# Last ten MLP blocks: layer one in 49 products for 1280 tokens at a time, layer two summed in four steps

## The chip, the cores and the metric

The kernel runs on one NeuronCore of one Trainium2 chip. The metric is the device time of the core in microseconds (us). The kernel before took 1379.85 us, the median of three runs (1377.99 to 1382.92). Engine names in the profile: PE is TensorE (PEld its weight loads), DVE VectorE, ACT ScalarE, POOL GpSimd, SP SyncE, which here issues DMAs.

## The reference

Two blocks follow each other, all in float32. The first is attention over 8 batches, 8 heads, 576 positions and 64 dimensions per head, in which scores below the row's maximum less tau are dropped:

```python
scores = scale * np.matmul(q, k.transpose(0, 1, 3, 2))
thresh = np.max(scores, axis=-1, keepdims=True) - tau
scores = np.where(scores >= thresh, scores, -1000000000.0)
...
attn = attn / (np.sum(attn, axis=-1, keepdims=True) + 1e-09)
return np.matmul(attn, v).astype(np.float32)
```

Its output, as 4608 tokens by 512, goes through a two-layer MLP with an exact gelu:

```python
h = x @ w_in                                   # 512 -> 2048
g = 0.5 * h * (1.0 + erf(h * inv_sqrt2))
return (g @ w_out).astype(np.float32)          # 2048 -> 512
```

## The kernel before

The tokens are cut into 18 blocks of 256 (TOK). Attention runs by pairs of heads, 32 pairs in all. Beside it, between the pieces of attention, the first eight blocks (PLAIN) go through the MLP with ordinary products: `block_steps` multiplies w_in by the block's x (L559), takes a gelu on ScalarE and multiplies by w_out (L573). x is held with the 512 model channels on the partitions, as four chunks c of 128; chunk c comes from the c-th pair of heads of a batch. `weigh_v` (L469) makes x from the attention weights and v, and `divide` (L502), on GpSimd, divides it by the softmax sums, whose reciprocals (inv) come back by DMAs that SP issues. Order is written out by hand (`manual_schedule`): each engine runs its instructions in the order in which the Python program issues them.

The last ten blocks run after attention, in `strassen` (L664). Five of them (AWAY, blocks 8 to 12) are finished early and are parked in DRAM by `put_away`, others stay in SBUF; `bring` loads a parked block back. Two blocks at a time (DUOS) go through both layers with seven products in place of eight (the scheme of Strassen in Winograd's form): each matrix is cut into 2 x 2 quarters, sums of quarters are multiplied, and the products are added up.

- Sums of w_in quarters (s1, s2, s4) are made once, on VectorE, before the stage (`weights_in`, L622, L633 to L635 and L641). Sums of x quarters (t1, t2, t4) are made for each pair on VectorE (`x_sums`, L659 to L662), those of w_out while the first pair runs (`w_out_sums`, L704 to L707).
- Layer one: for each of eight chunks j of 128 of the 1024 columns in a half of d_ff, seven products of two matmuls, 256 tokens wide. All matmuls of the stage are recorded at L693, in `product`. Products that belong together are added in one PSUM bank: the bank x takes m1, then m6, m5 and m3 on top, and after each of them ScalarE or VectorE copies the bank's state out before the next is added. The bank y takes m7 and then m4, the bank v_ takes m2.
- Gelu on ScalarE, then the sums gs1, gs2 and g11 - g21 on VectorE (`finish_chunk`).
- Layer two: the same seven products, each over all eight j, for two chunks m of 128 tokens, then DMAs of 128 x 256 to the output.

Both layers are float32; each matmul shows in the trace as two passes, a weight load and a matmul each. The x, w_in and w_out tiles are many tiles in pools before, and one tensor each after.

## Time and profile before

| what | value |
|---|---|
| median of three runs | 1379.85 us (1377.99 to 1382.92) |
| profiled execution: its own time, which is its span | 1380.0 us, 20235 instructions |
| mean granted TensorE clock | 0.995 |
| TensorE busy | 99% of the span |
| last ten blocks | 889.35 us to the end, 490.65 us |
| in these: TensorE, VectorE, ScalarE, GpSimd busy | 484.96, 149.36, 126.64, 1.69 us |
| one pair of blocks between two stalls | 96.97 us, 448 passes |

The page gives one profiled execution, on the one core. The span is all that the page shows of its time; it stands 0.15 us from the median of the runs. A duration of an operation is its busy time; engines other than TensorE start the next operation somewhat before the last one's end, so the pitch of two starts is shorter than the duration. The granted clock in the last ten blocks is 1.00.

### The profile page before, as it was taken

The page shows a single profiled execution, that of the slowest core. Times are in us where ns is not written, and L with a number is a line of the kernel's source. Part 1 is how long each engine was busy: PE and PEld are TensorE (multiplying, and loading weights), DVE is VectorE, ACT ScalarE, POOL GpSimd, SP SyncE. Part 2 cuts the span into 40 slices and gives each one's busy share as a digit, 9 for nine tenths or more (in the row PEclk, how much of TensorE's full clock was granted, in tenths as well). Part 3 has the DMA queues.
Part 4 walks back from the last instruction along what each step waited for, and adds up shares of the span by engine and source line. Part 5 has one row for each costly group of instructions (what it writes and reads, how often), then busy time and mean ns, then how long its engine had stood idle before and what let it go on. Part 6 is the DMA issues. An engine that isn't in the chain of part 4 may idle for free.

```text
span 1380.0 us, 20235 instructions
## 1 busy us (share of the span) xinstructions
PE 1361.4 (99%) x6734; PEld 971.0 (70%) x6734; DVE 892.6 (65%) x1740; ACT 638.0 (46%) x1160; POOL 435.6 (32%) x896
## 2 busy tenths in 40 slices
PE   9899999999999999999999999999999999999999
PEld 7677557466466566576475475588888888888887
DVE  7998777788888888888888888763142242241330
ACT  7766537448348358357367366241240230330420
POOL 5553344454554554554555551100000000000000
PEclk9999999999999999999999999999999999999999
DMA  9987366577677687787787775500000001001000
GB/s 295 313 301 222 80 162 140 139 167 175 157 176 171 157 198 163 161 213 158 167 219 156 169 180 116 111 0 8 23 1 27 19 1 47 15 0 54 9 8 23
DMA packets 215094, 169.19 MB, mean 123 GB/s; under 512 B 114176, under 2 KB 199488, under 8 KB 214992
## 3 DMA queue, kind: packets, MB, share of 16 engines
q1 hardware_dynamic: 191040, 112.84, 36.1%
q0 software_dynamic: 23520, 54.77, 13.1%
q8 instruction: 55, 0.90, 0.3%
q14 instruction: 47, 0.39, 0.1%
q10 hardware_dynamic: 432, 0.30, 0.1%
HBM read 72.73 MB, written 12.52 MB: 62 GB/s over the span
## 4 chain that ended last, share of the span: by engine, by line
PE 95%; DVE 2%; ACT 1%; DMA 1%; issue 0%; POOL 0%; ACTq 0%; DVEq 0%
PE bank L693 35%; PE hT L559 17%; PE o_ps L573 17%; PE sc L367 13%; PE xT L484 11%; PE tr L309 2%; DMA raw<-in_moe_w_in_dram 1%; DVE p L398 1%; ACT p L382 0%; DVE nmx L379 0%; DVE power L187 0%; DVE w_in L189 0%; PE tr L280 0%; ACT diag L412 0%; PE idle L125 0%
## 5 line engine op out<-in xcount | busy, mean ns | idle before, releaser
L382 ACT ACTIVATE p<-sc,nmx 128x576 f32<-128x576 f32 x288 | 201.8, 737 | 268.8 <-DVE nmx L379 268.7
L398 DVE SCALAR_TENSOR_TENSOR p<-sc,thr,p 128x576 f32<-128x576 f32 x288 | 225.4, 816 | 60.0 <-ACT p L382 58.8
L379 DVE TENSOR_REDUCE nmx<-sc 128x1 f32<-128x576 f32 x288 | 205.6, 751 | 66.2 <-PE sc L367 65.6
L559 PE MATMUL hT<-x,w_in 128*128 128x256 f32 x1024 | 241.1, 385 | 0.0
L573 PE MATMUL o_ps<-w_out,g 128*128 128x512 f32 x512 | 237.7, 605 | 0.0
L559 PEld LDWEIGHTS hT<-x,w_in 128*128 128x128 f32 x1024 | 189.8, 190 | 48.9 <-issue 23.5
L380 POOL TENSOR_SCALAR thr<-nmx,tau_eff 128x1 f32<-128x1 f32 x288 | 89.0, 309 | 390.4 <-DVE nmx L379 390.0
L573 PEld LDWEIGHTS o_ps<-w_out,g 128*128 128x128 f32 x512 | 93.5, 191 | 111.0 <-issue 109.4
L484 PE MATMUL xT<-pT,v 128*64 128x256 f32 (+1 forms) x1280 | 164.0, 409 | 0.2 <-issue 0.2
L367 PE MATMUL sc<-kT,qT 64*128 64x288 f32 x960 | 157.2, 431 | 2.4 <-DVE p L398 1.9
L445 DVE STREAM_TRANSPOSE turned_p<-p 128x1152 f32<-128x1152 f32 x112 | 154.4, 1378 | 3.9
L367 PEld LDWEIGHTS sc<-kT,qT 64*128 64x128 f32 x960 | 89.5, 187 | 75.7 <-issue 64.3
L484 PEld LDWEIGHTS xT<-pT,v 128*64 128x64 f32 x1280 | 89.1, 137 | 72.7 <-issue 13.3
L693 PE MATMUL bank<-x,w_in 128*128 128x256 f32 x480 | 116.7, 379 | 0.0
L693 PE MATMUL bank<-w_out,unit 128*128 128x256 f32 x520 | 115.5, 379 | 0.0
L234 POOL DMA_DIRECT2D v<-in_v_dram x208 | 110.9, 536 | 4.5 <-issue 2.5
L693 PEld LDWEIGHTS bank<-w_out,unit 128*128 128x128 f32 x520 | 98.9, 190 | 13.3
L693 PEld LDWEIGHTS bank<-x,w_in 128*128 128x128 f32 x480 | 91.3, 190 | 12.7 <-issue 0.5
L693 PE MATMUL bank<-v,unit 128*128 128x256 f32 x320 | 82.1, 379 | 0.0
L225 POOL DMA_DIRECT2D q<-in_q_dram x104 | 70.8, 686 | 10.0 <-issue 8.9
L693 PE MATMUL bank<-unit,turned_p 128*128 128x256 f32 x320 | 73.2, 379 | 0.0
L532 ACT ACT_TABLE_LOAD x56 | 71.8, 1283 | 1.0
(161 smaller groups left out, 1491.4 us busy)
## 6 DMA issues: line engine op xcount, KB each, us to landing
pT<-turned_p SPq DMA_DIRECT2D x448, 160.0 KB, 3.6
pT<-pd_tail SPq DMA_DIRECT2D x112, 80.0 KB, 2.9
q<-in_q_dram POOLq DMA_DIRECT2D x104, 72.0 KB, 3.7
k<-in_k_dram POOLq DMA_DIRECT2D x104, 72.0 KB, 3.1
inv<-turned SPq DMA_DIRECT2D x56, 128.0 KB, 4.0
v<-in_v_dram POOLq DMA_DIRECT2D x156, 40.0 KB, 3.2
x<-x SPq DMA_DIRECT2D x10, 512.0 KB, 4.5
raw<-in_moe_w_out_dram POOLq DMA_DIRECT2D x9, 512.0 KB, 4.4
```

The costliest lines, as they stand in the source:

```text
L234: eng.dma_start(t[r:P:4, e, 0:n, :], rows[:, r * KR:r * KR + n, :])
L367: nc.tensor.matmul(sc[e][:, h, 0:HALF], lhsT=lhsT, rhs=s["kT"][rows, at:at + HALF], start=True, stop=True)
L379: nc.vector.tensor_reduce(nmx[:, e:e + 1], sc, axis=AXIS.XY, op=ALU.max, negate=True)
L380: nc.gpsimd.tensor_scalar(thr[:, e:e + 1], nmx[:, e:e + 1], -1.0, tau_eff, op0=ALU.mult, op1=ALU.subtract)
L382: nc.scalar.activation(w[:, e * S:(e + 1) * S].rearrange("p (h s) -> p h s", h=2), sc, AF.Exp, bias=nmx[:, e:e + 1], scale=1.0)
L398: nc.vector.scalar_tensor_tensor(row, sc[e][:, :, 0:HALF], thr[:, e:e + 1], row, op0=ALU.is_ge, op1=ALU.mult, accum_out=den[e])
L445: nc.vector.transpose(turned_p[:, :, i // 2, 0:NB, i % 2 * Q:(i % 2 + 1) * Q], w.rearrange("p (e b i) -> p e b i", e=2, i=Q))
L484: nc.tensor.matmul(to, lhsT=s["v"][:, e, c, :], rhs=rhs, start=(c == 0), stop=(c == KR - 1))
L532: nc.scalar.activation(t, src, AF.Gelu)
L559: nc.tensor.matmul(hT[:, j % 2, :], lhsT=w_in_sb[c][:, j * P:(j + 1) * P], rhs=x_blk[n][:, c, :], start=(c == 0), stop=(c == N_DM - 1))
L573: nc.tensor.matmul(o[:, 0:d_model], lhsT=g[j][:, m * P:(m + 1) * P], rhs=w_out_sb[j], start=(j == 0), stop=(j == N_DF - 1))
L693: nc.tensor.matmul(to, lhsT=l, rhs=r, start=start and k == 0, stop=k == len(pairs) - 1, skip_group_check=not start)
```

## The change

The last ten blocks run in two groups of five (GROUPS: blocks 13 to 17, which are in SBUF, then the five parked ones). In each group, layer one goes two levels deep: each of the seven products of quarters is itself done by seven products of quarters of quarters, 49 in all. Each is one matmul: 128 channels, 128 columns of w_in, and 320 tokens, which lie in five runs of 64 (RUN), one from each block. d_ff is done in four steps j: in each, layer one makes 4 x 128 of the 16 x 128 hidden channels, and layer two multiplies them by their rows of w_out (seven products of two matmuls of 256 columns for each of five chunks of 128 tokens) and adds the result to `tail["o"]` in SBUF. After the fourth step the sums go to the output. So there are eight steps of 49 + 70 matmuls.

- `layer_in` does the seven outer products. R, U, V and W are the partial results of layer one; every one of the 49 products is taken out of PSUM by `taken`: a copy on ScalarE where nothing is to be added (8 of 49), else an add on VectorE of a tile in SBUF and the bank. The product of s1 and t1 is kept apart (T), and added to V (giving W) and to U on GpSimd (`m5_out`, `m5_all`).
- `chain` sets the order on TensorE: m1, m5 of the chain before, m7, m2, m3 of the chain before, m6, m4. The last chain of layer one has its m5 and m3 among the first products of `layer_out`.
- `sums(0)` and `sums(1)` are three VectorE operations each, of 640 columns, after the last gelus of a step.
- w_in sums: those of the first step are made on VectorE before the stage (`weights_first`), those of the others on GpSimd during the step before (16 operations). w_out sums (four operations) are made on GpSimd.
- x sums: `x_sums` gives 28 inner and four outer operations in a group; VectorE and GpSimd share them. Nine are issued before the first product, the others are put one by one between products (`beside`, `step`). At the switch of groups five DMAs on SP load the parked blocks, after the last reader of the old x.
- Pools: x, w_in and w_out become one tensor each with slots that the program gives out by hand; attention's tiles are freed in two parts, and the new tiles take their place.

The diff, cut to its core:

```diff
-    order = list(range(PLAIN + 5, N_BLK)) + AWAY
-    DUOS = list(zip(order[0::2], order[1::2]))
+    GROUPS = [list(range(PLAIN + 5, N_BLK)), AWAY]
...
+    NJ = 4
+    RUN = TOK // 4
+    QT = len(AWAY) * RUN
+    HT = 2 * QT
+    HD = d_model // 2
+    MT = HT // P
+    vec, pool = nc.vector, nc.gpsimd
...
+    w_in_q = w_in_all.rearrange("p (k h) (f g j i) -> p k h f g j i", k=2, f=2, g=2, i=P)
+    w_out_q = w_out_all.rearrange("p (f g j) d -> p f g j d", f=2, g=2)
+    def w_part(f, k, j):
+        return w_in_q[:, k, :, f, :, j, :]
+    def weights_first():
+        room = tail["room"] = early_end.enter_context(tc.tile_pool(name="wsum", bufs=1, side="right", reuse_waits="tile"))
+        tail["s"] = room.tile([P, 4, 2, 2, P], FP32, name="s_out")
+        tail["ss"] = room.tile([P, 4, 3, P], FP32, name="s_in")
+        tail["sp"] = room.tile([P, 3, 4, P], FP32, name="s_plain")
+        tail["t"] = room.tile([P, 4, 2, HD], FP32, name="t_out")
+        w_in_sums(vec, 0)
+    def w_in_sums(eng, j):
+        s, ss, sp = tail["s"], tail["ss"], tail["sp"]
+        def plain(n, *at):
+            to = [sp[:, n:n + len(at), k, :] for k in range(4)]
+            if len(at) == 1:
+                a = {(g, h): w_part(*at[0], j)[:, h, g, :].unsqueeze(1) for g in range(2) for h in range(2)}
+            else:
+                k = at[0][1]
+                a = {(g, h): w_in_q[:, k, h, :, g, j, :] for g in range(2) for h in range(2)}
+            add(eng, to[0], a[1, 0], a[1, 1])
+            sub(eng, to[1], to[0], a[0, 0])
+            sub(eng, to[2], a[0, 0], a[1, 0])
+            sub(eng, to[3], a[0, 1], to[1])
+        plain(0, (0, 0))
+        add(eng, s[:, 0], w_part(1, 0, j), w_part(1, 1, j))
+        sub(eng, s[:, 1], s[:, 0], w_part(0, 0, j))
+        sub(eng, s[:, 2], w_part(0, 0, j), w_part(1, 0, j))
+        sub(eng, s[:, 3], w_part(0, 1, j), s[:, 1])
+        a = {(g, h): s[:, :, h, g, :] for g in range(2) for h in range(2)}
+        add(eng, ss[:, :, 0, :], a[1, 0], a[1, 1])
+        sub(eng, ss[:, :, 1, :], ss[:, :, 0, :], a[0, 0])
+        sub(eng, ss[:, :, 2, :], a[0, 1], ss[:, :, 1, :])
+        sub(eng, a[1, 0], a[0, 0], a[1, 0])
+        plain(1, (0, 1), (1, 1))
+    def w_out_sums(eng, j):
+        t = tail["t"]
+        b11, b12 = w_out_q[:, 0, :, j, 0:HD], w_out_q[:, 0, :, j, HD:2 * HD]
+        b21, b22 = w_out_q[:, 1, :, j, 0:HD], w_out_q[:, 1, :, j, HD:2 * HD]
+        sub(eng, t[:, 0], b12, b11)
+        sub(eng, t[:, 1], b22, t[:, 0])
+        sub(eng, t[:, 2], b22, b12)
+        sub(eng, t[:, 3], b21, t[:, 1])
...
+    def x_sums():
+        room = list(tail["x_room"])
+        x = xall[:, 0:len(AWAY), :, :].rearrange("p b (k h) (o t) -> p b k h o t", k=2, o=2)
+        part = {f"b{k + 1}{o + 1}": x[:, :, k, :, o, :] for k in range(2) for o in range(2)}
+        right = tail["right"] = {}
+        def inner(eng, name, v, keep=False):
+            b = {(h, i): v[:, :, h, i * RUN:(i + 1) * RUN] for h in range(2) for i in range(2)}
+            t1, t2, t4 = (room.pop(0) for _ in range(3))
+            t3 = room.pop(0) if keep else b[0, 1]
+            right[name] = {"b11": b[0, 0], "b21": b[1, 0], "b22": b[1, 1], "t1": t1, "t2": t2, "t3": t3, "t4": t4}
+            yield eng, lambda: sub(eng, t1, b[0, 1], b[0, 0])
+            yield eng, lambda: sub(eng, t3, b[1, 1], b[0, 1])
+            yield eng, lambda: sub(eng, t2, b[1, 1], t1)
+            yield eng, lambda: sub(eng, t4, b[1, 0], t2)
+        def outer(eng, out, a, b):
+            yield eng, lambda: sub(eng, out, a, b)
+        t1, t2, t4 = tail["t_x"]
+        yield from inner(vec, "b11", part["b11"], True)
+        yield from outer(vec, t1, part["b12"], part["b11"])
+        yield from inner(vec, "t1", t1, True)
+        yield from outer(vec, t2, part["b22"], t1)
+        yield from outer(pool, part["b12"], part["b22"], part["b12"])
+        yield from outer(vec, t4, part["b21"], t2)
+        yield from inner(vec, "t2", t2)
+        yield from inner(vec, "t3", part["b12"])
+        for name, v in ("b21", part["b21"]), ("t4", t4), ("b22", part["b22"]):
+            yield from inner(pool, name, v)
...
+    def taken(to, x, first):
+        if first is None:
+            nc.scalar.copy(to, x)
+        else:
+            add(vec, to, first, x)
+    waiting = []
+    beside = []
+    def step(which):
+        if which is not None:
+            which()
+        if beside:
+            beside.pop(0)[1]()
+        while beside and beside[0][0] is pool:
+            beside.pop(0)[1]()
+    def chain(n, m, takes, done=None, runs=1):
+        x, y = bank("sc", n), bank("mm", n)
+        v = bank("mm", n) if "m2" in m else None
+        def one_of(name, to, start):
+            def run():
+                product(to.rearrange("p (b t) -> p b t", b=runs) if runs > 1 else to, m[name], start)
+                for t in takes[name]:
+                    taken(t[0], to, t[1])
+                if done:
+                    done(name)
+            return run
+        before = waiting.pop(0) if waiting else (None, None)
+        step(one_of("m1", x, True))
+        step(before[0])
+        step(one_of("m7", y, True))
+        if v is not None:
+            step(one_of("m2", v, True))
+        step(before[1])
+        step(one_of("m6", x, False))
+        step(one_of("m4", y, False))
+        waiting.append((one_of("m5", x, False), one_of("m3", x, False)))
...
+    def layer_in(j, between):
+        c, g = tail["c"], tail["g"]
+        R, U, V, W, T = c[:, 0], c[:, 1], c[:, 2], c[:, 3], g[:, 0]
+        def flat(t):
+            return t.rearrange("p a b c -> p (a b c)")
+        def outer(a, b, to, first, done=None):
+            l, r = left(a, j), tail["right"][b]
+            m = {"m1": ("a11", "b11"), "m2": ("a12", "b21"), "m3": ("s4", "b22"), "m4": ("a22", "t4"),
+                 "m5": ("s1", "t1"), "m6": ("s2", "t2"), "m7": ("s3", "t3")}
+            m = {k: [(l[p], r[q])] for k, (p, q) in m.items()}
+            def at(f, t, again=False):
+                d = to[:, f, t, :]
+                return d, (d if again else None if first is None else first[:, f, t, :])
+            takes = {"m1": [at(0, 0)], "m7": [at(1, 1)], "m6": [at(1, 0)], "m4": [at(1, 0, True)],
+                     "m2": [at(0, 0, True)], "m5": [at(1, 1, True)], "m3": [at(0, 1)]}
+            chain(QT, m, takes, done, len(AWAY))
+        def when(**what):
+            return lambda name: what[name]() if name in what else None
+        def m5_out(f, t):
+            return lambda: add(pool, W[:, f, t, :], V[:, f, t, :], T[:, f, t, :])
+        def m5_all():
+            m5_out(0, 1)()
+            add(pool, flat(U), flat(U), flat(T))
+        def sums(t):
+            g11, g21, g12, g22 = (z[:, :, t, :] for z in (R, U, V, W))
+            sub_first = g[:, 0, :, t, :], g[:, 1, :, t, :]
+            add(vec, sub_first[0], g21, g22)
+            sub(vec, sub_first[1], sub_first[0], g11)
+            sub(vec, g21, g11, g21)
+        outer("a11", "b11", R, None)
+        outer("s1", "t1", T, None)
+        between()
+        outer("s2", "t2", U, R)
+        outer("s3", "t3", V, U, when(m2=m5_out(0, 0), m4=m5_out(1, 0), m5=m5_out(1, 1), m3=m5_all))
+        outer("a12", "b21", R, R, when(m3=lambda: (gelu_on(flat(W)), gelu_on(flat(R)))))
+        outer("a22", "t4", V, V, when(m3=lambda: gelu_on(flat(V))))
+        last = {"m2": lambda: gelu_on(U[:, 0, 0, :]), "m4": lambda: (gelu_on(U[:, 1, 0, :]), sums(0)),
+                "m5": lambda: gelu_on(U[:, 1, 1, :]), "m3": lambda: (gelu_on(U[:, 0, 1, :]), sums(1))}
+        outer("s4", "b22", U, U, when(**last))
+    def layer_out(blocks, j, between):
+        c, g, t, o = tail["c"], tail["g"], tail["t"], tail["o"]
+        g11, g21, g12, g22 = (c[:, i].rearrange("p f t n -> p f (t n)") for i in range(4))
+        gs1, gs2 = (g[:, i].rearrange("p f t n -> p f (t n)") for i in range(2))
+        lo, hi = o[:MT], o[MT:]
+        first, final = j == 0, j == NJ - 1
+        def rows(z, m, w):
+            return [(z[:, f, m * P:(m + 1) * P], w[:, f]) for f in range(2)]
+        def w(k, d):
+            return w_out_q[:, k, :, j, d * HD:(d + 1) * HD]
+        def store(half, m):
+            for r in range(2):
+                q, b = divmod(2 * m + r, len(AWAY))
+                row = blocks[b] * TOK + (2 * half + q) * RUN
+                nc.sync.dma_start(out[row:row + RUN, :], o[half * MT + m][r * RUN:(r + 1) * RUN, :])
+        before = waiting.pop(0)
+        for m in range(MT):
+            v = bank("mm", HD)
+            def run(m=m, v=v):
+                product(v, rows(g12, m, w(1, 0)), True)
+                taken(lo[m][:, 0:HD], v, None if first else lo[m][:, 0:HD])
+            step(run)
+            if m < 2:
+                step(before[m])
+        between(-1)
+        beside.insert(0, (vec, lambda: sub(vec, g12, g12, gs2)))
+        for m in range(MT):
+            l0, l1, h0, h1 = lo[m][:, 0:HD], lo[m][:, HD:2 * HD], hi[m][:, 0:HD], hi[m][:, HD:2 * HD]
+            new = (lambda d: (d, None if first else d))
+            takes = {"m1": [(l0, l0)], "m7": [new(h1)], "m6": [new(h0)], "m4": [(h0, h0)], "m5": [(h1, h1)], "m3": [new(l1)]}
+            ms = {"m1": rows(g11, m, w(0, 0)), "m7": rows(g21, m, t[:, 2]), "m6": rows(gs2, m, t[:, 1]),
+                  "m4": rows(g22, m, t[:, 3]), "m5": rows(gs1, m, t[:, 0]), "m3": rows(g12, m, w(1, 1))}
+            def done(name, m=m):
+                if final and name == "m5":
+                    store(1, m)
+                if final and name == "m3":
+                    store(0, m)
+            chain(HD, ms, takes, done)
+            between(m)
+    def last_blocks():
+        assert set(x_free) == {XSLOTS - 2, XSLOTS - 1}
+        GROUPS[0].sort(key=x_at.get)
+        x_tiles()
+        beside.extend(x_sums())
+        for _ in range(9):
+            beside.pop(0)[1]()
+        w_out_sums(pool, 0)
+        steps = [(n, j) for n in range(len(GROUPS)) for j in range(NJ)]
+        for at, (n, j) in enumerate(steps):
+            after = steps[at + 1] if at + 1 < len(steps) else None
+            def in_layer_in():
+                if at:
+                    w_out_sums(pool, j)
+            def in_layer_out(m):
+                if after is None:
+                    return
+                if m == -1:
+                    if after[0] != n:
+                        for b, x in enumerate(GROUPS[after[0]]):
+                            nc.sync.dma_start(xall[:, b, :, :], away.pop(x))
+                    w_in_sums(pool, after[1])
+                if m == 1 and after[0] != n:
+                    beside.extend(x_sums())
+            layer_in(j, in_layer_in)
+            layer_out(GROUPS[n], j, in_layer_out)
+        while waiting:
+            for f in waiting.pop(0):
+                f()
+        assert not beside
...
-            ext = weights_in()
+            early_end.close()
+            weights_first()
...
-    strassen(*ext)
+    late_end.close()
+    last_blocks()
```

## The prediction

> **What bounds the kernel now.** I read the page first, then the chain in order of time, then the time table by windows over the last ten blocks, and last the single rows that price the new operations. The page's busy line, TensorE's and GpSimd's slices and the chain's shares:
>
> ```profile
> PE 1361.4 (99%) x6734; PEld 971.0 (70%) x6734; DVE 892.6 (65%) x1740; ACT 638.0 (46%) x1160; POOL 435.6 (32%) x896
> ...
> PE   9899999999999999999999999999999999999999
> ...
> POOL 5553344454554554554555551100000000000000
> ...
> PE 95%; DVE 2%; ACT 1%; DMA 1%; issue 0%; POOL 0%; ACTq 0%; DVEq 0%
> ```
>
> TensorE is the bound everywhere, and GpSimd does nothing in the last third. The chain from 889 us on, which is the part the change replaces:
>
> ```profile
> 937.51 96.97 PE bank L693 x448
> 1034.48 0.02 issue
> 1034.50 0.43 DVE turned_p L743
> 1034.94 0.04 issue
> 1034.98 96.97 PE bank L693 x448
> ```
>
> A pair of blocks is 448 passes (224 products, two passes each) in 96.97 us, 0.2165 us a pass of 256 columns, and one stall of 0.50 us. The stage runs from 889.35 to 1376.9, 487.5 us. Nothing else is in its way: only fewer passes, or new stalls, can move it.
>
> **Passes.** Layer one had 112 products a pair, 560 in all, 256 columns wide. It gets 49 in each of eight steps, 392, 320 columns wide. Layer two keeps 560 products of 256 columns (70 a step). A pass of 512 columns has a pitch of 0.43 in the weight loads:
>
> ```profile
> 888.06 0.19 PEld L573 LDWEIGHTS o_ps<-w_out,g 128*128 128x128 f32 x1 [0.24 <-issue]
> 888.49 0.19 PEld L573 LDWEIGHTS o_ps<-w_out,g 128*128 128x128 f32 x1 [0.24 <-issue]
> ```
>
> So 320 columns cost 0.2165 + 64 x (0.43 - 0.2165)/256 = 0.270 us. Layer one: 784 x 0.270 = 211.7; layer two: 1120 x 0.2165 = 242.5; together 454.2 against 5 x 96.97 = 484.9. **-30.7 us**, and the five stalls of 0.50 go: **-2.5**. The moving operand now lies in five runs of 64 columns; weigh_v already reads runs of 64 without loss (22 such passes of 320 columns, half the array wide, in 3.56 us at 880.61), so I add nothing.
>
> **Prices of the other engines**, VectorE and ScalarE:
>
> ```profile
> 895.06 0.42 DVE L704 TENSOR_TENSOR turned_p<-w_out 128x256 f32<-128x256 f32 x1
> 895.52 0.42 DVE L705 TENSOR_TENSOR unit<-w_out,turned_p 128x256 f32<-128x256 f32 x1
> 895.86 0.42 DVE L706 TENSOR_TENSOR w_out<-w_out,w_out 128x256 f32<-128x256 f32 x1
> ```
>
> ```profile
> L737 ACT ACTIVATE unit<-unit 128x256 f32<-128x256 f32 x40 | 16.7, 417 | 39.6 <-DVE unit L736 39.6
> ...
> L532 ACT ACTIVATE g<-g 128x512 f32<-128x512 f32 x6 | 3.2, 616 | 0.0
> ```
>
> VectorE: 0.42 for 256 columns, the next starts 0.34 later (0.46 if it reads the result); with 512 columns 0.68 and 0.61. That is 1.05 ns a column: 320 columns 0.49 (pitch 0.41), 640 columns 0.82 (0.74), 1280 columns 1.49 (1.41). ScalarE's gelu: 0.47 for 320, 1.2 for 1280. VectorE starts 0.2 to 0.3 after a product's end. Layer one is now evicted 49 times a step, 41 of them on VectorE: 41 x 0.49 + six half sums x 0.82 = 25 us of the 26.5 us that TensorE needs there. VectorE, 27.7 us busy in 97 before, has no slack left in this layer.
>
> **The seam between the layers**, once a step. (1) The first layer-two product reads V after one gelu of 1280 columns. Its last product ends, 0.25 + 0.49 for the eviction and 1.25 for the gelu follow; TensorE has two products (1.08) to do. Stall 1.0. (2) From the end of that gelu, ScalarE does the next (0.47), VectorE the three sums of the first half (0.85 + 0.74 + 0.74), which stand in its queue ahead of two evictions (0.34, 0.49): 3.7. TensorE has v0, m5, v1: 2.3; then m3 needs the bank that m5's eviction frees. Stall 1.4. (3) After m3: eviction 0.7, gelu 0.47, three sums 2.4, four evictions 1.4: 5.0, against five products, 4.3: 0.7 to 0.8. Next to it the subtract of 1280 columns (1.41) stands ahead of m7's eviction, and m4 waits 0.8. Together 4.0 a step; in the two first steps of a group ScalarE takes layer two's evictions, and 2.1 remain. 6 x 4.0 + 2 x 2.1 = 28, and some 30 restarts at 0.1 (the first product after a stall took 1.13 instead of 1.03): **+31**.
>
> **Start and switch of groups.** GpSimd's last products of attention are late already, and DMAs on SP (inv) end their wait:
>
> ```profile
> 889.69 1.69 POOL L507 TENSOR_TENSOR x<-x,inv 128x64 f32<-128x64 f32 x3 [16.33 <-DMA inv<-turned]
> ```
>
> They end 2.0 us after the stage's start. The old first pair did not need them; t2 of the new first group does, and VectorE's queue stops there with the evictions behind it. GpSimd's rate is 728 ns for 256 columns and 320 for 64, 2.1 ns a column: 0.86 for 320, 1.27 for 512, 2.9 for 1280. Behind the divides it has four layer-two weight sums (5.1) and then b22-b12 (2.9), done at 10.0; two t3 sums that need it stand on VectorE ahead of m5's eviction (11.7 when read). TensorE has work until 4.8. **+6.8**. At the switch five DMAs of 512 KB go out on SP ahead of the stores; one lands in 3.8 to 4.5 us, and some 14 us lie before the first reader, so five in a row just fit; 19 more VectorE operations in three chains cost **+2**. The stores are 40 as before, now all in the fourth step of each group; the last ones: **+0.5**. Moved weight sums and put-away blocks before the stage: fewer VectorE operations there than now, and TensorE is the bound: 0.
>
> Without any conflict between engines: 1380.0 - 30.7 - 2.5 + 31 + 6.8 + 2 + 0.5 = **1387**.
>
> **GpSimd beside VectorE.** GpSimd, idle here before, now gets sixteen w_in sums (up to 1.27 each), four w_out sums and five adds a step, and VectorE does sums with both operands in SBUF at the same moments. What the trace shows of that, first GpSimd, then VectorE:
>
> ```profile
> 39.55 0.31 POOL L380 TENSOR_SCALAR thr<-nmx,tau_eff 128x1 f32<-128x1 f32 x1 [2.52 <-DVE nmx L379]
> 40.13 0.66 POOL L380 TENSOR_SCALAR thr<-nmx,tau_eff 128x1 f32<-128x1 f32 x1 [0.27 <-DVE nmx L379]
> ```
>
> ```profile
> 39.93 0.70 DVE L189 SCALAR_TENSOR_TENSOR w_in<-w_in,power 128x512 f32<-128x512 uint32 x1
> ```
>
> The same one-column operation takes 0.29 (its median) beside a reduction, and 0.66 when it starts inside a VectorE operation with two SBUF operands: it ends 0.16 after that one. Beside L398, with one operand in PSUM, L507 keeps its 728 ns (724 with VectorE idle). So evictions do not conflict, sums of two SBUF tiles do, and GpSimd waits to their end. The reverse, VectorE waiting for GpSimd, no row shows. Bounds: nothing; or the rest of GpSimd's operation at each sum, or two operations if GpSimd's next one gets in first. In the seam: the first three sums start 0.2, 1.27, 1.27 late (2.7), the second three 2.1, so 4.7 a step, in the seven steps that have w_in sums after them: 33. At the start t2, t4 and five inner sums alternate with GpSimd's: +7; at the switch +7. That is 47; I take off the fixed 0.18 us of each GpSimd operation (its row at zero columns), a sixth: **+39**. I take this near-full value because the wait seen is to the end of the other's operation, which is exclusive use and not sharing. Sum: 1387 + 39 = **1426**, against a profiled execution of 1380.0 whose median of runs is 1379.85, the same within 0.2.
>
> The Trainium skill ("SBUF — State Buffer", section "Who interferes with whom") says that VectorE and GpSimd share one read/write port pair under an exclusive lock, that a VectorE instruction with two SBUF inputs contends with a GpSimd one that reads SBUF, and that whichever starts first keeps it for its whole length. The rows above agree for the side they show. By this rule the sum is 1387 + 47 = 1434; by those rows alone, which show VectorE never held, 1387.
>
> **Rivals.** A: VectorE is not held: 1387, still slower, since the seam eats the saving; for it, no row has VectorE waiting. B: GpSimd's queue, always full there, wins twice for each sum: 1387 + 2 x 39 = 1465; against it, the one place in the trace where both queue up goes the other way: a GpSimd operation that starts at 135.62 takes 0.84 us and lets two of VectorE's pass. C, the other side: the seam is covered, because gelus and sums end while TensorE still has products queued. Then 1380 - 33.2 + 9.3 + 12 (hold at start and switch) = 1368. It decides below 1.5 us a step (12/8), where I count 4.0 unheld. For it: the stage before hides all its sums but 0.5 us a pair; against it: the gelu's 1.25 us alone exceeds two products. D: the work is not what it says: excluded by the order of instructions, 49 and 70 products a step.
>
> **Numbers.** Main case 0.60, between 1403 and 1450; A 0.19 (1381 to 1400, stalls 20% off either way); B 0.12; C 0.09. The range 1381 to 1465 leaves out C and the upper half of B. A measurement here tells 0.3% (4 us) from no change. Faster is C, 0.09; same the low end of A, 0.06; slower 0.85.
>
> **What would show it.** Right: 784 layer-one passes at 0.27; in each step VectorE sums of 640 columns idle before them on GpSimd or ending late, longest at the seam; TensorE waits of 3 to 4 us for VectorE at m3 and 2 to 3 at m6; steps near 65 us, the last near 61. Sums back to back at 0.74 beside busy GpSimd mean A. Wrong if layer one's passes differ from 0.27, if evictions with a PSUM operand are slowed too, or if the five loads are late.

## The result, and the profile after

| | before | after |
|---|---|---|
| median of four runs | 1380.71 us (1377.99 to 1382.92) | 1432.74 us (1431.63 to 1434.21) |
| ratio of the runs | | 1.0378, 95% interval 1.0362 to 1.0394 |
| span of the profiled execution | 1380.0 | 1429.8 |
| passes in the last ten blocks | 2240 | 1904 |
| last ten blocks, first pass to end of span | 490.65 | 541.78 |
| mean granted clock | 0.995 | 0.982 |

The changed kernel is 3.8% slower; 1426 had been predicted. The page of after, first its busy line, then TensorE's, GpSimd's and the clock's slices, and the shares of the chain:

```profile
PE 1353.3 (95%) x6398; PEld 911.7 (64%) x6398; DVE 1106.9 (77%) x2040; ACT 600.2 (42%) x1000; POOL 683.4 (48%) x1106
...
PE   9899999999999999999999999698989888989898
...
POOL 5553455455455554555545512836261657344330
PEclk9999999999999999999999999899999999999999
...
PE 80%; DVE 12%; ACT 3%; DMA 2%; issue 1%; SPq 1%; POOL 0%; ACTq 0%; DVEq 0%; POOLq 0%
```

TensorE has 336 passes fewer and is busy only 8 us less, mostly because passes at a lower clock, which follow below, are longer. GpSimd's zeros at the end are gone but for the last slice, and VectorE, 2% of the chain before, is 12% of it. The place is the seam between the layers. First the chain of after in a regular step (start, duration, work; L666 is the helper that adds, L663 the one that subtracts), then the same stretch of the last step, beside which GpSimd has no w_in sums to make:

```profile
1054.27 0.50 DVE c L666
...
1055.39 1.64 ACT c L834 x2
...
1057.05 0.87 DVE g L666
...
1057.95 1.78 DVE g L663
1059.72 1.80 DVE c L663
1061.52 0.33 DVE o L666
1061.86 0.41 DVE c L666
...
1064.17 1.05 DVE g L666
...
1065.24 1.77 DVE g L663
1067.01 1.27 DVE c L663
1068.28 1.32 DVE o L666 x4
1069.60 1.98 DVE c L663
1071.58 0.34 DVE o L666
```

```profile
1390.18 0.83 DVE g L666
...
1391.04 0.82 DVE g L663
1391.86 0.74 DVE c L663
...
1395.25 0.84 DVE g L666
...
1396.11 0.83 DVE g L663
1396.93 0.74 DVE c L663
...
1398.99 1.40 DVE c L663
```

It is the same list of operations: a gelu, three sums of the first half, the two evictions that stood behind them (0.33 and 0.41), then three sums of the second half, evictions, and the subtract of 1280 columns. Between the two steps the sums differ by 0.04, 0.96, 1.06, then 0.21 (the second half's first sum, 1.05 against 0.84), 0.94, 0.53 and 0.58: 4.3 us together. The evictions are equal. GpSimd makes its w_in sums at the same moments, two of them here (start, duration, operation):

```profile
1057.19 1.85 POOL L663 TENSOR_TENSOR s_out<-w_in,s_out 128x512 f32<-128x512 f32 x1
1059.12 1.73 POOL L666 TENSOR_TENSOR s_in<-s_out 128x512 f32<-128x512 f32 x1
```

A table of the loss shows what became of each term. Take from the time between the first passes of two steps the time of the passes in it at the pitches seen where TensorE doesn't wait (0.269 us for 320 columns, 0.216 for 256). What remains is waiting, and passes at a slower clock. A wait, here and below, is counted from the moment when the next pass would have come at its pitch; the profile's idle time, in brackets in its lines, is 0.16 us shorter, since it begins where the pass before ends:

| loss against unhindered passes, us | predicted | after |
|---|---|---|
| start of the stage | 6.8 + 7 x 5/6 = 12.6 | 14.5 |
| seam of the first step of a group | 2.1 + 0.4 + 3.9 = 6.4 | 6.3 and 5.8 |
| seam of steps 2, 3, 4 | 4.0 + 0.4 + 3.9 = 8.3 | 8.4 each |
| seam of steps 6 and 7 | 8.3 | 9.0 and 11.4 |
| seam of the last step (not held), stores | 4.4 + 0.5 | 4.1 + 0.8 |
| switch of groups | 2 + 7 x 5/6 = 7.8 | 5.9 + 1.3 |
| together, before rounding | 79.3 | 84.1 |

In the row of the prediction 0.4 is a step's share of the restarts, and 3.9 a step's share of the hold (4.7 less a sixth). The part that nothing had predicted is the clock. Windows of after, columns us, busy time and number of each engine, then the granted clock; the first is the start of the stage, the second a seam, the third the stretch up to the next seam, the fourth that seam:

```profile
888.06:905.00 16.94, 5.05 (x20) 3.28 (x18) 14.63 (x12) 2.67 (x6) 16.23 (x12) 0.73 0.05 17
...
990.00:1001.80 11.80, 7.88 (x27) 5.61 (x26) 9.85 (x12) 2.88 (x5) 11.04 (x8) 0.86 0.00 0
1001.80:1055.00 53.20, 51.47 (x215) 40.40 (x214) 34.48 (x73) 6.10 (x11) 17.88 (x19) 1.00 0.00 1
1055.00:1066.70 11.70, 7.77 (x26) 5.57 (x25) 9.75 (x12) 2.89 (x5) 10.93 (x8) 0.85 0.00 0
```

In the records of the clock, the stage of after has nine stretches at half rate behind its long waits: of 3.41 us in six cases, of 6.83 in two and of 13.65 at the start. Passes in them come about every 0.43 us, and they took 17.7 us more than at full rate; 66.4 of the 84.1 us are waits. Before has full clock in the whole stage up to its last microsecond.

### The profile page after: what moved, and what is told of

Read it like the earlier page. It is cut to its first block, busy times and chain, and to the rows that moved or that the text cites. A ratio compares the mean times of both kernels' runs of the same rounds, so it can differ in the third digit from the quotient of the medians.

```text
span 1429.8 us, 20064 instructions
## 1 busy us (share of the span) xinstructions
PE 1353.3 (95%) x6398; PEld 911.7 (64%) x6398; DVE 1106.9 (77%) x2040; ACT 600.2 (42%) x1000; POOL 683.4 (48%) x1106
## 4 chain that ended last, share of the span: by engine, by line
PE 80%; DVE 12%; ACT 3%; DMA 2%; issue 1%; SPq 1%; POOL 0%; ACTq 0%; DVEq 0%; POOLq 0%
PE bank L781 27%; PE o_ps L611 16%; PE hT L596 14%; PE sc L403 12%; PE xT L520 10%; DVE c L663 2%; DVE g L663 2%; ACT c L834 1%; DVE o L666 1%; PE tr L345 1%; DVE g L666 1%; DVE x L663 1%; DVE c L666 1%; DVE p L434 1%; DVE nmx L415 1%
## 5 line engine op out<-in xcount | busy, mean ns | idle before, releaser
L596 PE MATMUL hT<-xall,w_in 128*128 128x256 f32 x1024 | 241.1, 385 | 0.0
L596 PEld LDWEIGHTS hT<-xall,w_in 128*128 128x128 f32 x1024 | 189.5, 190 | 49.2 <-issue 23.9
L666 DVE TENSOR_TENSOR o<-o,bank 128x256 f32<-128x256 f32 x240 | 98.4, 418 | 106.8 <-PE bank L781 105.8
L666 DVE TENSOR_TENSOR c<-c,bank 128x320 f32<-128x320 f32 x304 | 147.3, 487 | 40.0 <-PE bank L781 27.1
L781 PE MATMUL bank<-w_out,c 128*128 128x256 f32 x480 | 131.7, 409 | 12.0 <-ACT c L834 6.9
L781 PEld LDWEIGHTS bank<-w_out,c 128*128 128x128 f32 x480 | 98.3, 207 | 35.9 <-ACT c L834 10.9
L834 ACT ACTIVATE c<-c 128x320 f32<-128x320 f32 (+1 forms) x56 | 44.6, 811 | 141.4 <-DVE c L666 73.1
L792 ACT COPY c<-bank 128x320 f32<-128x320 f32 x32 | 13.6, 426 | 196.9 <-PE bank L781 196.8
L663 POOL TENSOR_TENSOR t_out<-w_out 128x512 f32<-128x512 f32 x16 | 21.5, 1345 | 146.2 <-PE bank L781 146.2
L781 PE MATMUL bank<-t_out,c 128*128 128x256 f32 x320 | 84.9, 389 | 6.5 <-DVE o L666 6.5
```

The source lines that it names most:

```text
L596: nc.tensor.matmul(hT[:, j % 2, :], lhsT=w_in_sb[c][:, j * P:(j + 1) * P], rhs=x_blk[n][:, c, :], start=(c == 0), stop=(c == N_DM - 1))
L663: eng.tensor_tensor(out, a, b, op=ALU.subtract)
L666: eng.tensor_tensor(out, a, b, op=ALU.add)
L781: nc.tensor.matmul(to, lhsT=l, rhs=r, start=start and k == 0, stop=k == len(pairs) - 1, skip_group_check=not start)
```

## The experiments

Three questions were put. Does VectorE wait for GpSimd, and for which of its operations? How much of a step's loss is the hold, and how much the order in VectorE's queue? What brings the half clock, and what does it cost? The theory was that of the prediction (order of the queue, and on top of it the hold). The rivals were that the order alone explains it, and that GpSimd is only a bystander.

**A stream of GpSimd operations beside the kernel before.** 400 additions of 128 columns, then 400 memsets, into a tile that nobody reads:

```diff
+    def stream():
+        for _ in range(400):
+            nc.gpsimd.tensor_tensor(probe, w_in_sb[0][:, 0:P], w_in_sb[1][:, 0:P], op=ALU.add)
+        for _ in range(400):
+            nc.gpsimd.memset(probe, 0.0)
```

> The kernel before, with GpSimd, idle there in the last ten blocks, running 400 additions of two SBUF tiles of 128 columns (0.457 us each, about 185 us from the stage's start) and then 400 memsets of 128 columns, which only write. Hold theory: while the additions run, VectorE's sums of two SBUF tiles (L716, L717, L718, L765; 0.42 us now) take longer or start later, by up to 0.46 us each, and GpSimd's additions get longer too; VectorE's adds with one operand in PSUM (L736, L740, L743) stay at 0.42; under the memsets all are at 0.42 again. The total moves by less than 5 us, since VectorE has slack here. Rival (the engines do not disturb each other, the seam alone is slow): L716 to L718 stay at 0.42 throughout. Second rival (any GpSimd work slows VectorE): L736 and L740 get longer too, and the memsets do it as well.

It took 1381.51 us, against 1381.71 for the kernel before beside it. Groups of VectorE's operations (line, operation, tiles and shapes, count, busy time, mean ns), first while the additions ran (889 to 1090 us), then while the memsets ran (1118 to 1215):

```profile
L774 DVE TENSOR_TENSOR unit<-unit,turned_p 128x256 f32<-128x256 f32 x16 | 9.3, 644 | 3.0 <-PE bank L702 3.0
...
L752 DVE TENSOR_TENSOR unit<-unit,bank 128x256 f32<-128x256 f32 x13 | 5.5, 421 | 5.7 <-PE bank L702 5.7
L727 DVE TENSOR_TENSOR unit<-pd_tail,unit 128x256 f32<-128x256 f32 x8 | 5.4, 674 | 0.0
```

```profile
L774 DVE TENSOR_TENSOR unit<-unit,turned_p 128x256 f32<-128x256 f32 x8 | 3.4, 425 | 2.3 <-PE bank L702 2.2
...
L752 DVE TENSOR_TENSOR unit<-unit,bank 128x256 f32<-128x256 f32 x6 | 2.5, 421 | 2.7 <-PE bank L702 2.7
...
L727 DVE TENSOR_TENSOR unit<-pd_tail,unit 128x256 f32<-128x256 f32 x4 | 1.7, 418 | 0.0
```

That answers the first question, and it is the row which the trace of before lacked. A VectorE sum of two SBUF tiles takes 0.644 or 0.674 us beside GpSimd additions and 0.425 or 0.418 beside memsets; an eviction with one operand in PSUM takes 0.421 beside both. The delay, 0.22 to 0.26 us, is about half of one GpSimd addition (0.479 here). Over all 108 sums of 256 columns beside the additions the mean is 0.61 and the longest 0.715, so none is delayed by as much as one whole addition. This fits VectorE waiting for the rest of the GpSimd operation that is under way. The Trainium skill ("SBUF — State Buffer", section "Who interferes with whom") has the same three cases: contention with GpSimd's reads, none with its mere writes, none for a VectorE operation with a single SBUF input. The rows here agree with all three. No TensorE wait came of it, since the queue of before has room.

**Waits of rising length in the kernel before.** VectorE gets 5, 10, 15, 20 and 25 additions of 128 columns ahead of one eviction, once in each pair of blocks:

```diff
+                if j == NJ - 1:
+                    for _ in range(5 * sb + 5):
+                        vec.tensor_tensor(extra, w_in_sb[0][:, 0:P], w_in_sb[1][:, 0:P], op=ALU.add)
```

> The kernel before, with 5, 10, 15, 20 and 25 more VectorE additions of 128 columns ahead of the eviction on which TensorE waits once a pair (0.7 us now). Each addition is estimated at 0.21 to 0.33 us, so the five stalls become some 1.7 to 2.4, 2.8 to 4, 3.8 to 5.6, 4.9 to 7.3 and 6 to 9 us. Clock theory: where the stall is over some 3 us, one or two stretches of 3.41 us at half the granted clock follow, and passes of 256 columns then come every 0.43 in place of 0.216, which costs up to 1.7 us for each stretch; the shortest stall has none. Total 1380 + 16 to 27 of stalls + 3 to 10 of slow clock. Rival (the slow stretches of the changed kernel belong to its work, not to its stalls): no stretch at half clock in this stage.

The time was 1410.33 us. TensorE waited 1.65, 3.28, 4.90, 6.52 and 8.15 us. The second and the third wait in TensorE's timeline (start, duration, operation; in brackets the idle time before it), and windows from the clock's records behind them:

```profile
1036.59 1.81 PE L695 MATMUL bank<-x,unit 128*128 128x256 f32 x4 [3.12 <-DVE turned_p L748]
...
1139.97 2.07 PE L695 MATMUL bank<-x,unit 128*128 128x256 f32 x4 [4.74 <-DVE turned_p L748]
```

```profile
936.50:939.90 3.40, 3.38 (x16) 3.00 (x17) 2.58 (x7) 0.80 (x2) 0.00 (x0) 1.00 0.00 0
1036.90:1040.30 3.40, 3.40 (x9) 2.66 (x8) 1.19 (x3) 0.47 (x2) 0.00 (x0) 0.50 0.00 0
1139.30:1146.20 6.90, 6.23 (x15) 4.97 (x16) 1.80 (x5) 0.80 (x2) 0.00 (x0) 0.51 0.00 0
```

Four passes that take 1.03 us elsewhere take 1.81 and 2.07 here. Behind the wait of 1.65 the clock stays full (16 passes in 3.4 us), behind that of 3.28 it is half for 3.41 us (9 passes), and for 6.83 behind each of the longer ones. GpSimd is idle in all of this, so it is TensorE's standing still that comes ahead of the half clock. The extra operations cost 24.8 us of waits and 9.1 us of slow passes. The Trainium skill ("TensorE: Matmul & The Clock Gate", section "Part 1: The HAM clock gate (the "warmup" mystery)") describes a free-running activity window of 3413 ns, after an idle one of which the clock is halved. The lengths here are one and two such windows. The whole of a window need not be idle, however: a wait of 3.28 sufficed here, and in after waits of 3.2 did. How much of it must be idle is worked out in the last section.

**The change without the w_in sums of the later steps.** They are left out, so layer one uses the first step's sums throughout and the output is another:

```diff
-                    w_in_sums(pool, after[1])
+                    pass
```

> The changed kernel with the w_in sums of steps two to eight left out (GpSimd does not make them; the sums of the first step are used again, so the output is not the reference's). Hold theory: in all steps the second and third of VectorE's half sums fall back from 1.78 and 1.8 to 0.82 and 0.74, as they already are in the last step; the wait at m3 falls from 3.2 to 1.2 us and the ones at chain 0 from 2.05 to 1.5, so 2.5 us a step in seven steps, 18 us, and the stretches at half clock at these seams go with the long stalls, up to 10 us more: 1405 (1400 to 1415). Rival (the seam is slow by its own queue): 1430 or more.

1401.31 us (1398.61 to 1404.02), ratio 1.0141 (1.0092 to 1.0190): 31 us less than after, against the 1405 expected. VectorE's sums in after, from 889 us on, and in this kernel:

```profile
L663 DVE TENSOR_TENSOR g<-g,c 128x640 f32<-128x640 f32 x16 | 26.5, 1655 | 0.6
L663 DVE TENSOR_TENSOR c<-c 128x640 f32<-128x640 f32 x16 | 24.2, 1511 | 0.0
L663 DVE TENSOR_TENSOR c<-c,g 128x1280 f32<-128x1280 f32 x8 | 15.0, 1880 | 0.0
```

```profile
L663 DVE TENSOR_TENSOR g<-g,c 128x640 f32<-128x640 f32 x16 | 13.2, 825 | 0.5
L663 DVE TENSOR_TENSOR c<-c 128x640 f32<-128x640 f32 x16 | 13.1, 818 | 0.0
L663 DVE TENSOR_TENSOR c<-c,g 128x1280 f32<-128x1280 f32 x8 | 11.9, 1484 | 0.0
```

Every sum is back at the price of before's rows (0.82 and 1.49), and the loss of a regular step falls from 8.4 to 4.1. The hold by the w_in sums costs 4.3 us a step, and this is the sum of the seven differences in the chains above.

**The change with the same sums made later.** A one-column GpSimd operation that reads the seam's last sum stands ahead of them, except at the switch:

```diff
+                    if after[0] != n:
+                        w_in_sums(pool, after[1])
+                if m == 0 and after[0] == n:
+                    late = tail["c"][:, 2, 1, 1, QT - 1:QT]
+                    sub(pool, tail["gate"], late, late)
                     w_in_sums(pool, after[1])
```

> The changed kernel, complete, but GpSimd starts the w_in sums of the next step only when VectorE's last sum of the seam is done (a one-column operation that reads its result stands ahead of them); at the switch of groups they stay where they were. Hold theory: as without these sums in six of seven steps, if the 15 to 19 us of them still end before the next step: 1432.7 - 15 - 8 = about 1410 (1403 to 1418). Rival (the seam's own queue): 1432. If the sums come too late for the next step, a new wait at its start, and up to 10 us more.

1408.88 us (1406.62 to 1411.13), ratio 1.0196 (1.0154 to 1.0238); 1410 had been expected. Six of the seven seams that had the hold lose what they lose without these sums, 4.1 each (2.0 in the first steps of the groups). The one at the switch, which is not gated, keeps its hold. So it is the place of the sums that costs, and not their amount.

**Another order at the seam, w_in sums where they were.**

```diff
-        outer("a22", "t4", V, V, when(m3=lambda: gelu_on(flat(V))))
+        v_done = {"m2": (0, 0), "m4": (1, 0), "m5": (1, 1), "m3": (0, 1)}
+        outer("a22", "t4", V, V, lambda name: gelu_on(V[:, v_done[name][0], v_done[name][1], :]) if name in v_done else None)
...
-        last = {"m2": lambda: gelu_on(U[:, 0, 0, :]), "m4": lambda: (gelu_on(U[:, 1, 0, :]), sums(0)),
-                "m5": lambda: gelu_on(U[:, 1, 1, :]), "m3": lambda: (gelu_on(U[:, 0, 1, :]), sums(1))}
+        last = {"m2": lambda: gelu_on(U[:, 0, 0, :]), "m4": lambda: gelu_on(U[:, 1, 0, :]),
+                "m5": lambda: (gelu_on(U[:, 1, 1, :]), [f() for f in sums(0)]), "m3": lambda: gelu_on(U[:, 0, 1, :])}
+        tail["late"] = sums(1)
...
-        beside.insert(0, (vec, lambda: sub(vec, g12, g12, gs2)))
+        beside[:0] = [(vec, f) for f in late]
```

(`sums` returns its three operations, and a place in the order without a product no longer takes one of the operations put between products; `late` holds those of the second half and the subtract in two halves, one to be made with each product.)

> The changed kernel with another order of VectorE's and ScalarE's work at the seam, nothing else: V's gelu in four pieces, each behind the eviction that ends its part; the sums of the first U inputs after m5's eviction instead of ahead of it; the sums of the second half and the subtraction of S2 spread one for each product over the next eight products. GpSimd's w_in sums stay where they were. The order theory (most of a step's stall is queueing ahead of m5's eviction, and the hold by GpSimd only lengthens what stands in that queue): the step's terms of 1.03, 3.2 and 0.7 go, a part of the last term of 1.34 stays, so some 5 us of 6.3 in seven steps and 2 to 4 in the others, about 35 us of stalls; the stretches at half clock that followed the 3.2 us stalls go with them (about 13 of 17.7 us), the one at the start stays: 1433 - 35 - 8 to 13 = 1385 to 1395. The hold theory (with the sums still beside GpSimd's, they come late wherever they stand, 1.7 us each where they took 0.8): only the order's unheld part of 3.7 a step goes, the hold's 2.5 a step stays as a wait on the sums in the next chain: 1433 - 27 - 4 = about 1402. Without any effect of the order: 1433.

1403.21 us (1400.06 to 1406.15), ratio 1.0171 (1.0155 to 1.0187). This is the 1402 of the hold theory. A regular step loses 4.2, all of it now in layer two: the gelu's and m5's waits are gone, and the sums, of which two are still held to 1.77 and 1.89 us, come late for the evictions behind them there.

**Both.** The order of the last run, and the w_in sums in two parts, the second behind a gate after chain 1.

```diff
-                    w_in_sums(pool, after[1])
+                    w_in_sums(pool, after[1], 0)
+                if m == 1:
+                    late = tail["c"][:, 2, 1, 1, QT - 1:QT]
+                    sub(pool, tail["gate"], late, late)
+                    w_in_sums(pool, after[1], 1)
```

> The order of the run before together with the w_in sums of the next step held back until the seam's last sum is done (the two halves of them at two places). Both theories agree that the steps' stalls are then gone but for about half a microsecond each, and that only the start (12 us and one stretch at half clock) and the switch (5 to 10 us) are left: stalls of about 20 us, slow clock 3 to 5 us, 452.8 us of passes, 5 us at the end: a stage of 482 to 486 us and a time of 1370 to 1376, against 490.7 us and 1381 before. If the order and the hold don't add (the order alone covers what the hold lengthens), this run equals the one before it within 3 us.

1379.87 us (1375.83 to 1383.33, ten runs), ratio 0.9993 (0.9981 to 1.0006). TensorE's waits in one regular step, first of after (1030.6 to 1095.6 us), then of this kernel (1020.6 to 1078.1):

```profile
PE bank L781 <- DVE c L666: 3.1, 1, 3.1
PE bank L781 <- DVE o L666: 1.7, 2, 1.2
PE bank L781 <- ACT c L834: 0.9, 1, 0.9
```

```profile
PE bank L785 <- DVE o L666: 0.5, 1, 0.5
```

In that step the first part of the w_in sums ends at 1047.28 us, before the seam's first sum begins at 1047.73, and all the seam's sums are back at 0.82. The loss of a regular step in the kernels that between them have both orders and both places of the sums:

| | w_in sums beside the seam | w_in sums behind it, or none |
|---|---|---|
| order of the change | 8.4 | 4.1 |
| sums behind the evictions, gelu in pieces | 4.2 | 0.9 |

The two causes are worth 3.2 to 4.3 us a step each, and add to all but 1.0 us (4.2 and 4.3 alone, 7.5 together). The stage is 485.5 us in the profiled execution, as expected, and 5.1 us shorter than before's; the time is that of before all the same, 4 us above the band expected. The stage began at 893.9 us, and in before at 889.35. In the eight profiles with the new stage it began between 886.9 and 893.9, in before and its two variants between 887.4 and 889.35. From 560 us on ScalarE waits 6.4 us here, 1.7 in before, for the DMAs that park x blocks in DRAM. That doesn't settle it: in after it waits 6.3, and the stage begins at 888.06, earlier than in before. Whether the change moves the start or chance does is open.

**The sums of x at the start in another order, and later.** VectorE makes inner sums only when the products that read them are near; GpSimd makes the first step's w_out sums after those of x.

```diff
-        yield from outer(pool, part["b12"], part["b22"], part["b12"])
-        yield from outer(vec, t4, part["b21"], t2)
         yield from inner(vec, "t2", t2)
+        yield from outer(vec, part["b12"], part["b22"], part["b12"])
         yield from inner(vec, "t3", part["b12"])
+        yield from outer(vec, t4, part["b21"], t2)
...
-        w_out_sums(pool, 0)
+        tail["hold"] = 4
+        beside.extend((pool, f) for f in w_out_sums(pool, 0, True))
```

> The kernel of the run before, and at the start of the stage the sums of x begin four products later in another order (those that the first outer products read come first, the sums of w_out for the first step behind them). If the start's 12 us are VectorE's and GpSimd's queue of sums (the order theory), about 6 us of them go, and the clock stays full there (2 to 3 us more): 5 to 9 us less than the run before, 1365 to 1370. If the start is bound by the amount of sums and not by their order: no difference.

1376.17 us (1372.49 to 1379.16, twelve runs), ratio 0.9969 (0.9958 to 0.9979), 3.7 us less than the run before it; 5 to 9 had been expected. The first wait, 9.6 us there, became three of 1.0, 1.7 and 0.7, but a new one of 6.5 us came at 923.8. Its cause stands in GpSimd's row of waits, 10.9 us for t_x: its sums of b21 wait for VectorE's T4, which I had put last. There T4 also reads T2 after an inner sum has been written over it, so the output of this kernel is another.

**Work for TensorE inside the wait.** The changed kernel with five extra products ahead of m3:

```diff
+                for _ in range(fill.get(name, 0)):
+                    product(spare[:, 1, 0:n].rearrange("p (b t) -> p b t", b=runs), m["m1"], True)
                 product(to.rearrange("p (b t) -> p b t", b=runs) if runs > 1 else to, m[name], start)
...
-        outer("s4", "b22", U, U, when(**last))
+        outer("s4", "b22", U, U, when(**last), {"m3": 5})
```

> The changed kernel with five extra products ahead of m3 of the last chain in every step (operands that are ready, results into a PSUM bank that nobody reads): 2.7 us of TensorE work inside the wait of 3.2 us, so that TensorE doesn't stand still there; what m3 waits for is as before. If the half clock is the answer to TensorE's standing still (theory), the seven or eight stretches of 3.41 us that follow m3's wait go, the one at the start and those at the switch stay: slow clock 17.7 -> 4 to 6 us. Of these 12 to 13 us the time shows all, if nothing else is late (1420), or only a part, if VectorE's queue is what the following passes then meet (the waits behind m3, 0.7 and 1.34, would grow by up to the 1.6 us that a stretch took: 1431). If the half clock has another cause (GpSimd's or VectorE's work beside it), the stretches stay, and the time is 1433 or above by the fillers at half rate.

1445.73 us (1443.99 to 1448.96), ratio 1.0479 (1.0464 to 1.0494): slower than after by 13 us, and far from the 1420 to 1431 that I had expected if the clock theory holds. In the profiled executions 9.2 of the 13 lie in the stage; it began 3.1 us later, too. TensorE around the seam in after, then in this kernel:

```profile
993.21 1.03 PE L781 MATMUL bank<-w_out,c 128*128 128x256 f32 x4
997.30 0.81 PE L781 MATMUL bank<-xall,s_in 128*128 128x320 f32 x2 [3.06 <-DVE c L666]
997.94 5.30 PE L781 MATMUL bank<-w_out,c 128*128 128x256 f32 x16
```

```profile
997.14 2.85 PE L781 MATMUL bank<-xall,s_out 128*128 128x320 f32 x10
999.83 0.70 PE L781 MATMUL bank<-xall,s_in 128*128 128x320 f32 x2
1000.37 3.62 PE L781 MATMUL bank<-w_out,c 128*128 128x256 f32 x16
1003.82 1.03 PE L781 MATMUL bank<-t_out,c 128*128 128x256 f32 x4
1008.43 2.08 PE L781 MATMUL bank<-t_out,g 128*128 128x256 f32 x4 [3.58 <-DVE o L666]
```

The theory of the clock holds at the place itself: with TensorE at work the clock stays full, and 16 passes take 3.62 us instead of 5.30. But nothing is won. The wait moves to the next operand that VectorE owes, 3.7 us where after has 0.7 and 1.3, and the half clock follows it there, at 1007.9 us, beside passes that nothing else delays. Extra products, waits and slow passes up to there cost 7.6 us a step, as against 8.4 in after, and the half clock behind it brings a regular step to 9.6 us or more. So through the seam VectorE's queue sets the time. After itself shows this in step 7, where no half clock follows m3's wait: the 16 passes take 3.62 us there too, the wait behind them grows from 0.7 to 2.4, and the seam's last wait ends 41.38 us into the step, against 41.37 in step 3 with its slow passes. So in after the stretch of slow passes, some 1.6 us, lay beside that queue; only where a stretch outlasts it does it cost, at the start (2.4 us) and in steps 6 and 7, where the clock was half for 6.83 us.

**The sums at the start in the right order.** T4 directly behind T2 (the edit is against the run with the sums in another order):

```diff
+        yield from outer(vec, t4, part["b21"], t2)
         yield from inner(vec, "t2", t2)
         yield from outer(vec, part["b12"], part["b22"], part["b12"])
         yield from inner(vec, "t3", part["b12"])
-        yield from outer(vec, t4, part["b21"], t2)
...
-        tail["hold"] = 4
+        tail["hold"] = 3
```

> The kernel of e7 with the sum T4 = B21 - T2 made ahead of T2's inner sums, one of which is written over T2 (in e7 it came behind them and read what they had left, so that e7's output is not the reference's; its time is read rightly), and the sums of x three instead of four products late. GpSimd's wait for that sum (10.9 us in e7) goes, and with it the 6.5 us stall that ended at 923.8; the third outer product gets its sums 1.5 us later. Stalls at the start 7 to 8 us instead of 9.9, at the switch 5 to 6 instead of 3: the stage 479 to 482 us, the time 1373 to 1377, 0.2 to 0.5% under the kernel before. If the start is bound by the amount of sums alone: as e7, 1376.

1373.21 us (1371.09 to 1377.21), ratio 0.9952 (0.9938 to 0.9966), the one kernel that computes the reference and beats both: 0.5% under before, 4.2% under after. GpSimd's wait for t_x is 3.3 instead of 10.9 us. Start and first step lose 10.2 us, the step with the switch 7.2 and a regular step 0.9. With T4 last these were 13.2 and 4.3, so the switch takes back what the start gains: the stage is 481.8 us long, against 481.1. The 3 us between the medians of the two kernels match the stage's start in their profiles (890.6 and 893.6), whose cause is open.

## Why the prediction was right, and where it was not

- **Passes.** 784 at 0.270 and 1120 at 0.2165, 454.2 us. Measured 0.269 and 0.216, 452.8. The five runs of 64 columns cost nothing.
- **The seam without conflict.** 4.0 a step and 2.1 in the first steps, found by laying VectorE's queue beside TensorE's products. Where the w_in sums are absent or late: 4.1, and 2.0 to 2.1. Shown, with the restarts of 0.1 already in it, which the prediction had added once more (3 us). With the hold, the signs that it named came: steps of 65.0 us, the last of 61.4, and a wait of 3.2 at m3; behind m3 the waits are 0.7 at m6 and 1.3 at m4, where it named 2 to 3 at m6.
- **GpSimd beside VectorE.** The one term that no row had shown, and the one that decided between 1387 and 1426. That VectorE is held is shown by the first run, and that it costs by those without the w_in sums and with them late. Of 3.9 us a step it takes 4.3: the six sums 2.1 and 1.7, as priced (4.7 less a sixth; its own 2.7 and 2.1 make 4.8, which is under 1 us over the stage), and 0.6 for the subtract of 1280 columns, which the prediction had forgotten to hold. Rival A, in which VectorE doesn't wait, falls. B falls too: beside the additions no sum is delayed by a whole GpSimd operation (0.29 at most, of 0.479), and at the seam the delays of 0.96 and 1.06 stay under one of 1.27. By the skill's rule the sum was 1434, by the prediction's rebate 1426; the stage's 84.1 us lie between the 79.3 and 87.3 of the two, with a clock in it that neither had.
- **C, the covered seam.** It decides below 1.5 us a step without the hold, and there the seam costs 4.1. The runs with another order and late w_in sums show that it was reachable, at 0.9, but not by the change's order.
- **Start and switch.** 12.6 and 7.8 were forecast, 14.5 and 7.1 came. The start's wait alone was 12.05; 2.4 are half clock. At the start VectorE was held as the prediction has it: two inner sums of 320 columns, which begin at 898.14 beside GpSimd's 1280-column subtract of b12, take 4.2 us together, where one costs 0.49 in the prices.
- **The step that failed: no term for the clock.** The prediction took passes at full rate in every part of the sum, because the stage of before shows 1.00 throughout. After, 17.7 us of slow passes are in the stage. That this moved the result by little is luck of place: in the regular seams they lie beside VectorE's queue, as step 7 shows. What is left of them, some 2.4 us at the start and 3.6 in steps 6 and 7, is more than the 4.8 us between 79.3 and 84.1; the double count of the restarts and the shorter switch take the rest back.
- **Span for time.** The prediction set the profiled execution's span equal to the time. Each run's time is 1.7 to 2.1 us above its span (1431.63 against 1429.8), so some 2 of the 6.7 us missed were never in the kernel; before's span of 1380.0 belonged to a run above its median. Of the rest 1.1 is the median's distance from the profiled run, and some 3.8 are in its span: 4.8 more of waits and slow passes, 1.6 more behind the last pass (4.7 us against before's 3.1), less 1.4 for cheaper passes and 1.3 because the stage began earlier.

## What to carry to other kernels

Price a sum by what runs beside it: a VectorE operation on two SBUF tiles beside GpSimd arithmetic cost up to the rest of one GpSimd operation more, 0.82 turned into 1.78 here, while evictions from PSUM cost the same. Look for the point where an eviction that TensorE waits for queues behind such sums, and put both apart: the sums behind the eviction, and GpSimd's work behind the sums. A saved product is worth nothing while the new order leaves the queue on the way (452.8 us of passes took 541.8), and the same products gave back the time of before only after both were moved, and a gain of 0.5% with the sums at the start reordered as well.

## What the hardware showed that I had not expected

- TensorE's granted clock fell to one half in stretches that begin and end on a raster of 3.41 us: in after the starts 933.55, 998.41, 1063.26 and 1128.11 lie 19 such lengths apart. What counts is how long TensorE stands idle within one window of the raster, and not how long a wait is. In the stages of the eleven profiles each of the 33 windows at full clock with 2.04 us of idle time or more was followed by half clock, and none of those with 1.85 or less was.
- So in the kernel without w_in sums an idle time of 3.23 us, which ended at 1136.33 and fell 1.5 and 1.7 us deep into two windows, brought no half clock, and one of 2.08, which ended at 1143.86 and lay in a single window, brought 3.41 us of it. An added wait can cost more or less half clock by where it falls.
- Keeping TensorE busy with useless products kept the clock at 1.00 in that place, and the kernel became 13 us slower, 9.2 of them in the stage.
- GpSimd is held too: its sums of 512 columns at the seam take 1.73 to 1.85 us, where others of that width take 1.27.
